# A gated recurrence and an FFT-like convolution: the small spectrum's eviction, the order of the filter's loads, and a planner's priorities

## The chip, the cores and the metric

The kernel runs on one core of one Trainium2 chip. A core has five engines with queues of their own: TensorE (PE in the profile; weight loads are PEld) multiplies matrices and writes into PSUM, VectorE (DVE) and ScalarE (ACT) work elementwise and empty PSUM, GpSimd (POOL) works elementwise on SBUF, and SyncE (SP) here only issues DMA transfers. The metric is the time of one execution on the device in microseconds (us), less being better; of several runs the median is given.

## The reference

Two layers follow each other. Inputs are `x` and `f_logit` of shape (4, 6272, 256), and all results are float32.

```python
# first layer: a gated recurrence over time, per channel
f = lower_bound + (1 - lower_bound) * sigmoid(f_logit)
h[t] = f[t] * h[t-1] + (1 - f[t]) * x[t]          # 6272 steps, 4 x 256 channels
# second layer: projections, a circular convolution along time, gating
proj = h @ w_proj                                  # 256 -> 768
x1, x2, x3 = proj[..., :256], proj[..., 256:512], proj[..., 512:]
conv = irfft(rfft(x2) * rfft(filter_fft))          # length 6272, circular
out  = (x1 * conv * x3) @ w_out                    # 256 -> 256
```

## The kernel before, in words

The transform of length 6272 = 49 x 128 is done as matmuls in two factors. The kernel has a stage that prepares constants and the filter's spectrum, and then for each of the four batches a chain of phases. All names below are the kinds by which the code calls its operations.

**Preparation (`prepare`).** The filter (6.4 MB) is loaded in 13 groups (`ff`, L612) into places that later hold other things: seven in X2, two in Hu, one in the W region of HA and two in the A region of HA, where the constants are also built. Each group is copied to a rounding type (`fr`, L333 here: ScalarE), rotated by a matmul (`rot`, L623) and evicted (`f2`, L338 here: VectorE). When all 13 are there, the first factor `FF1` (L645) runs for 16 units, its results are evicted (`afs`), the second factor `FF2` (L663) follows, is evicted (`hw`, L335) and stored as the spectrum H in DRAM (`hst`, L671). One row of each unit is treated apart: it is collected in `mX` (L654), transformed by `last` (L680) and evicted once by another `hw` (L340) into eight spare columns, 49 to 56, of each of the 128 blocks of 113 columns in X2. This is the small spectrum, Hm. W, the projection and output weights, is loaded (`wl`, L475 and L477) into parts of HA that later hold the wrapped copy of h, and is scaled and copied on ScalarE (L481, L486, L491). The arguments of all constants are computed on VectorE and go through one sine on ScalarE (L563). `warm` matmuls keep TensorE running at the start.

**The recurrence (`hgrn`),** per batch in 13 chunks of 512 steps: load f_logit and x (`load`, L361; three buffers each), sigmoid (`sig`, L364, ScalarE), product (`u`, L366, GpSimd), transposes on TensorE (`sT` and `uT`, L373), the gate `f` (L387 ScalarE, L389 VectorE) and the scan (L395, VectorE). The first 3072 steps of h are copied behind its end (`wrap`, L343).

**The convolution,** per batch: `P` (L703) projects to x2, evicted into X2 (`x2`, L338 and L333). `F1` (L716) multiplies blocks of X2 and is evicted (`A`). `F2` (L761) is multiplied with H, which is loaded anew for each of 16 units (`H`, L751, three buffers), by `prod` (L774, VectorE). `mini` (L732), `zm` (L738, reads Hm) and `slot` (L766, GpSimd) do the row treated apart. `I2` (L784) goes back and is evicted as Th. Beside this, `x13` (L422), `xs` (L434) and `z` (L438, GpSimd) make x1 times x3. Then `I1` (L817), `y` (L823), `proj` (L835), `o` (L335) and `store` (L845) finish 13 groups of the output.

**What sets the order.** The order of all instructions, their engine where two can do it, and their PSUM banks are fixed before the run by the planner (`Plan`). It goes through the operations as a simulation would, with costs written in the code, and always takes the one that can start first; among those it takes the one with the highest level, which is the longest path to the end plus a number from the table `LEAD` for its kind and batch. `SHY` adds hundredths of a microsecond to the start for one engine, and so says which of two engines is preferred. A transfer lands, for the planner, at issue plus `lag` plus `dma`. Every engine then works through its own list in that order; an instruction waits until what it needs is there.

Of the kernel before, what the change touches and what calls it, by code (L numbers as in the profile page):

```python
# [24 lines left out]
Q = 49  # L25
TB = 98
# [11 lines left out]
NU = NEP // UE  # L38
HS = 64.0 / S
# [17 lines left out]
class Plan:  # L57
# [14 lines left out]
    SHY = {("A", "ACT"): 12, ("A", "DVE"): 22, ("Th", "ACT"): -16, ("Th", "DVE"): 1259,  # L72
            ("afs", "ACT"): 15, ("afs", "DVE"): 27, ("args", "ACT"): -138, ("args", "DVE"): 197,
            ("f", "ACT"): -6, ("f", "DVE"): 55, ("f2", "ACT"): 1138, ("f2", "DVE"): -715,
            ("fr", "ACT"): -88, ("fr", "DVE"): 39, ("fr", "POOL"): 1220, ("hw", "ACT"): -64,
            ("hw", "DVE"): -15, ("o", "ACT"): -63, ("o", "DVE"): 1089, ("tabs", "DVE"): -1060,
            ("tabs", "POOL"): -660, ("wcol", "DVE"): 109, ("wcol", "SP"): -513,
            ("wrap", "ACT"): 847, ("wrap", "POOL"): 90, ("x2", "ACT"): 88, ("x2", "DVE"): 19}
# [4 lines left out]

    LEAD = {
        "A": (5, -88, -65, 49), "F1": (101, -181, 3729, -100), "F2": (143, -28, -46, -324),
        "FF1": (15, 0, 0, 0), "FF2": (-324, 0, 0, 0), "H": (-141, 0, -2, -160),
        "I1": (0, -79, -343, -1), "I2": (-27, -52, 104, -101), "P": (142, 279, -78, 130),
        "Th": (-154, 45, -110, -124), "W": (-40, 0, 0, 0), "afs": (1, 0, 0, 0),
        "args": (-199, 0, 0, 0), "f": (236, 71, 103, 350), "f2": (-8, 0, 0, 0),
        "ff": (110, 0, 0, 0), "fr": (17, 0, 0, 0), "hst": (-231, 0, 0, 0), "hw": (36, 0, 0, 0),  # L90
        "iden": (188, 0, 0, 0), "iota": (11, 0, 0, 0), "last": (-216, 0, 0, 0),
        "load": (50, 16, 0, 117), "mX": (6, 0, 0, 0), "mini": (32, -33, -31, 2),
        "o": (-13, -109, 26, 170), "pad": (-72, 0, 0, 0), "pre": (-1, 0, 0, 0),
        "prod": (22, -43, 224, -263), "proj": (-5176, -5169, -102, -470), "rest": (4, 0, 0, 0),
        "rot": (7, 0, 0, 0), "sT": (-19, -534, 184, -2177), "scan": (-8, -139, -462, -1078),
        "sig": (175, 0, -1697, 1), "slot": (180, -88, 29, 529), "store": (123, 47, -49, 43),
        "tabs": (9, 0, 0, 0), "turns": (-99, 0, 0, 0), "u": (13, 9, -123, -140),
        "uT": (-126, -29, -3660, 551), "warm": (117, 0, 0, 0), "wcol": (-49, 0, 0, 0),
        "wl": (626, 0, 0, 0), "wrap": (-165, -168, -149, -144), "x13": (-30, -3595, -282, -1865),
        "x2": (-23, 7, 7, -169), "xs": (244, -309, 414, -35), "y": (37, 82, -119, -74),  # L100
        "z": (-639, -96, -92, 0), "zm": (662, -21, 80, 112),
# [6 lines left out]
    def op(self, kind, cost, fn, r=(), w=(), dma=0.0, lag=0.0, table=None, take=0, src=None, part=None):  # L108
        preds = set()
        for t in r:  # L110
            if t in self.writer:
                preds.add(self.writer[t])
        for t in w:
            if t in self.writer:
                preds.add(self.writer[t])
            preds.update(self.readers.get(t, ()))
        me = len(self.ops)
        if src is not None:
            preds.add(src)
            self.ops[src]["users"].append(me)  # L120
        self.ops.append(dict(kind=kind, batch=self.batch, cost=cost, fn=fn, preds=preds, dma=dma, lag=lag,
                             table=table, succ=[], take=take, src=src, part=part, users=[]))
        for p in preds:
            self.ops[p]["succ"].append(me)
        for t in r:
            self.readers.setdefault(t, set()).add(me)
        for t in w:
            self.writer[t] = me
            self.readers[t] = set()
        return me  # L130
# [12 lines left out]
    def schedule(self, level):  # L143
# [3 lines left out]
        dma, table, rows, lanes = 0.0, "none", False, []  # L147
# [23 lines left out]
        uses, done, order = {}, {}, []  # L171
        while base:
# [35 lines left out]
            end[i] = t  # L208
# [20 lines left out]
        return max(end), order  # L229
# [9 lines left out]

    def emit(self):  # L240
        level = [v + self.LEAD.get(o["kind"], (0,) * 4)[o["batch"]] for v, o in zip(self.levels(), self.ops)]
        for i, e, b in self.schedule(level)[1]:
            if b is None:
                self.ops[i]["fn"](e)
            else:
                self.ops[i]["fn"](e, b)
# [3 lines left out]
def kernel(  # L250
# [101 lines left out]
    def hgrn(b):  # L352
        for c in range(NCHK):
# [6 lines left out]
            for dst, src, t in ((ft, f_logit, ("ft", k)), (xt, x, ("xt", k))):  # L360
                op("load", {"SP": 0.46}, lambda e, dst=dst, src=src, t0=t0, n=n: nc.sync.dma_start(  # L361
                    dst, src[b, t0:t0 + n, :].rearrange("(p j) d -> p j d", p=128)),
                   w=[t], dma=0.38 * nb, lag=2.4)
# [81 lines left out]
    def prepare(tmp):  # L445
# [4 lines left out]
        raws += [(HA[:, A0 + a:A0 + a + 2048], [("At", i), ("At", i + 1)]) for i, a in ((0, 0), (2, 2048))]  # L450
# [224 lines left out]
        def last(e, pb):  # L675
# [8 lines left out]
        op("hw", {"DVE": 1.5}, lambda e, pb: copy(  # L684
            e, Hm[:TB],
            PS[:TB, pb:pb + 2].rearrange("p e (a k i) -> p e a k i", a=2, k=2), HS),
# [60 lines left out]
    def unit(b, u):  # L747
# [5 lines left out]
           r=[("H", u, i) for i in range(2)], w=[("Hu", h)], dma=1.7, lag=2.0)  # L753
# [50 lines left out]
    def phase_o(b):  # L804
        for g, r0 in enumerate(range(0, Q, 4)):
# [25 lines left out]
            def proj(e, ob, yk=yk, rn=rn):  # L831
# [16 lines left out]
               r=[("osb", k)], dma=0.37 * rn, lag=1.3)  # L848
# [58 lines left out]
```

## Time and profile before

| | |
|---|---|
| median of three runs | 513.89 us (512.42 to 514.6) |
| profiled execution, its own time | 517.71 us |
| span of its profile | 515.7 us |
| busy in the span: PE, DVE, ACT, POOL | 481.4, 450.7, 411.5, 370.5 us |
| mean granted TensorE clock | 0.985 |
| DMA traffic | 116.39 MB, mean 226 GB/s |
| FF1 starts, P of batch 0, F1 of batch 0 | 30.12, 85.12, 104.94 us |
| P of batches 1, 2, 3 starts | 202.14, near 312.4, 421.61 us |

Busy shares are averages over stages with different limits; a stage is read in its own window. Matmuls are pipelined, so a busy TensorE need not be at its peak. A wait is named by the instruction that ended it.

### The profile page before, as it was taken

What the parts mean: (1) busy time and instruction counts of PE and PEld (TensorE: products, weight loads), DVE (VectorE), ACT (ScalarE), POOL (GpSimd) and SP (SyncE); (2) the same over time, 40 slices, a digit from 0 to 9 for tenths busy, and PEclk for the clock granted to TensorE, in tenths of its full rate; (3) what the DMA queues carried; (4) which work ended last, traced back from release to release, by engine and by line L of the source; (5) the groups of instructions that cost most, each with busy time, mean ns of one, the idle gap of its engine ahead of it and who ended that gap; (6) DMA issues with size and microseconds to landing.
All of it is one profiled execution on the core that took longest, in us unless ns stands there. A gap on an engine that the chain in (4) does not pass through costs nothing.

```text
span 515.7 us, 13281 instructions
## 1 busy us (share of the span) xinstructions
PE 481.4 (93%) x5257; PEld 378.8 (73%) x5257; DVE 450.7 (87%) x465; ACT 411.5 (80%) x586; POOL 370.5 (72%) x315
## 2 busy tenths in 40 slices
PE   7997998789999899999999999999999999999796
PEld 5876777666776699867667888676777987666585
DVE  7985898989999799999998997988899989989754
ACT  4995887558988987789999877999987755999554
POOL 3475875449989973599999849699996632989800
PEclk9998999989999999999999999999999999999889
DMA  8979898326667899448658996247599860344157
GB/s 305 406 240 307 275 352 292 126 67 200 205 187 242 289 316 344 172 132 274 201 173 308 332 329 265 106 156 209 173 251 292 329 245 12 107 137 136 32 215 286
DMA packets 41725, 116.39 MB, mean 226 GB/s; under 512 B 4384, under 2 KB 6304, under 8 KB 41664
## 3 DMA queue, kind: packets, MB, share of 16 engines
q1 hardware_dynamic: 41664, 115.56, 65.3%
q8 instruction: 41, 0.67, 0.5%
q14 instruction: 20, 0.16, 0.1%
HBM read 84.54 MB, written 31.00 MB: 224 GB/s over the span
## 4 chain that ended last, share of the span: by engine, by line
PE 42%; DVE 9%; DMA 9%; POOL 8%; ACT 7%; issue 4%; POOLq 0%; ACTq 0%; DVEq 0%
PE PS L422 9%; PE PS L835 7%; PE PS L373 7%; POOL zt L438 6%; PE PS L784 5%; DVE X L338 5%; PE PS L716 5%; PE PS L761 4%; DMA XT<-in_x_dram 4%; PE PS L817 3%; DMA FL<-in_f_logit_dram 2%; DMA out_dram<-osb 2%; POOL XT L366 1%; DVE PP L774 1%; DMA Hu<-H 1%
## 5 line engine op out<-in xcount | busy, mean ns | idle before, releaser
L438 POOL TENSOR_TENSOR zt<-x1s,x3s 128x490 f16<-128x490 f32 (+1 forms) x104 | 200.6, 1950 | 47.4 <-ACT x3s L434 32.9
L774 DVE TENSOR_TENSOR PP<-PS,Hu 98x1008 f16<-98x1008 f32 x128 | 146.7, 1199 | 8.3 <-PE PS L761 3.3
L366 POOL TENSOR_TENSOR XT<-XT,FL 128x1024 f32<-128x1024 f32 (+1 forms) x52 | 117.0, 2253 | 48.0 <-DMA XT<-in_x_dram 18.9
L395 DVE TENSOR_TENSOR_SCAN HA<-fTs,HA,PS 128x512 f16<-128x512 f32 (+1 forms) x96 | 114.2, 1204 | 9.8 <-ACT fTs L387 6.0
L422 PE MATMUL PS<-HA,W 128*128 128x490 f16 (+1 forms) x416 | 106.4, 369 | 2.8 <-ACT x1s L434 1.0
L387 ACT ACTIVATE fTs<-PS,nomc 128x512 f32<-128x512 f32 (+1 forms) x99 | 66.3, 675 | 11.9 <-PE PS L373 11.3
L823 DVE TENSOR_TENSOR ys<-PS,zt 128x1024 fp32r<-128x1024 f32 (+1 forms) x52 | 59.6, 1161 | 14.1 <-PE PS L817 6.5
L335 ACT ACTIVATE osb<-PS 128x1024 f32<-128x1024 f32 (+1 forms) x52 | 50.7, 976 | 26.3 <-PE PS L835 23.7
L434 ACT ACTIVATE x1s<-PS 128x490 f32<-128x490 f32 (+1 forms) x104 | 61.0, 586 | 11.7 <-POOL zt L438 8.9
L373 PE MATMUL PS<-iden,XT 128*128 128x128 f32 x392 | 62.7, 281 | 2.2 <-POOL XT L366 0.6
L835 PE MATMUL PS<-Wo,ys 128*128 128x256 f32 x392 | 61.0, 299 | 3.5 <-DVE ys L823 3.2
L364 ACT ACTIVATE FL<-FL 128x1024 f32<-128x1024 f32 (+1 forms) x52 | 52.7, 1013 | 14.1 <-DMA FL<-in_f_logit_dram 13.9
L373 PE MATMUL PS<-iden,FL 128*128 128x128 f32 x392 | 61.3, 277 | 1.6 <-ACT FL L364 1.0
L434 ACT ACTIVATE x3s<-PS 128x490 f32<-128x490 f32 (+1 forms) x104 | 61.3, 589 | 1.2 <-PE PS L422 0.8
L784 PEld LDWEIGHTS <-PP 98*128 98x128 f16 x1024 | 51.1, 98 | 11.8 <-issue 2.8
L422 PEld LDWEIGHTS <-W 128*128 128x128 f16 x416 | 35.0, 98 | 30.0 <-issue 10.7
L835 PEld LDWEIGHTS PS<-Wo,ys 128*128 128x128 f32 x392 | 51.2, 194 | 7.0 <-DVE ys L823 3.4
L338 DVE CAST X<-PS 128x1024 f16<-128x1024 f32 (+1 forms) x38 | 51.4, 1461 | 4.6 <-PE PS L703 4.4
L333 ACT CAST Th<-PS 128x784 f16<-128x784 f32 x64 | 52.5, 821 | 3.0 <-PE PS L784 2.5
L333 ACT CAST HA<-PS 128x1024 f16<-128x1024 f32 x46 | 46.6, 1026 | 9.5 <-PE PS L716 9.3
L784 PE MATMUL PS<-VA,PP 98*128 98x98 f16 x512 | 52.7, 207 | 1.2 <-DVE PP L774 1.0
L373 PEld LDWEIGHTS PS<-iden,XT 128*128 128x128 f32 x392 | 44.4, 141 | 12.3 <-issue 2.2
(99 smaller groups left out, 697.2 us busy)
## 6 DMA issues: line engine op xcount, KB each, us to landing
Hu<-H SPq DMA_DIRECT2D x64, 392.0 KB
FL<-in_f_logit_dram SPq DMA_DIRECT2D x48, 512.0 KB
XT<-in_x_dram SPq DMA_DIRECT2D x48, 512.0 KB
out_dram<-osb SPq DMA_DIRECT2D x48, 512.0 KB
X<-in_moe_filter_fft_dram SPq DMA_DIRECT2D x7, 512.0 KB
H<-Hu SPq DMA_DIRECT2D x16, 196.0 KB
H<-Hu SPq DMA_DIRECT2D x16, 128.0 KB
HA<-in_moe_filter_fft_dram SPq DMA_DIRECT2D x3, 512.0 KB
```

The costliest lines, as they stand in the source:

```text
L333: nc.scalar.copy(dst, src)
L338: nc.vector.tensor_copy(dst, src)
L366: op("u", {"POOL": 0.1 + 0.553 * nb}, lambda e, xt=xt, ft=ft: nc.gpsimd.tensor_tensor(xt, xt, ft, op=AOP.mult), r=[("ft", k)], w=[("xt", k)])
L373: nc.tensor.transpose(PS[:, p, j:128 * nb:nb], src[:, j, cols], iden[:])
L387: nc.scalar.activation(fT, PS[:, p, 0:n], AF.Identity, scale=by, bias=1.0)
L395: nc.vector.tensor_tensor_scan(h, fT, PS[:, p, 0:n], init, op0=AOP.mult, op1=AOP.add),
L422: nc.tensor.matmul(PS[:, p, 0:n], W13[:, kh, js], HA[:, HB[kh] + t0:HB[kh] + t0 + n], start=(kh == 0), stop=(kh == 1))
L434: nc.scalar.activation(xs(i), PS[:, p, 0:n], AF.Copy, scale=1.0 if i else ZS),
L438: nc.gpsimd.tensor_tensor(late["zt"][:, jb, :, m0:m0 + nm], xs(0).rearrange("p (m r) -> p r m", r=Q), xs(1).rearrange("p (m r) -> p r m", ...
L774: nc.vector.tensor_tensor(PP[:TB, k, o, :, :, 1:64], px.unsqueeze(1).broadcast_to([TB, 2, UE, 63]), hh[:, :, :, 1:64], op=AOP.mult)
L784: nc.tensor.matmul(PS[:, ib + o, pr * TB:(pr + 1) * TB], PP[:TB, k, o, n, 2 * pr:2 * pr + 2, :], v[:TB], start=(n == 0), stop=(n == 1))
L835: nc.tensor.matmul(po[:, i, :], late["ys"][:, yk, kh, i * 128:(i + 1) * 128], Wo[:, kh, :], start=(kh == 0), stop=(kh == 1))
```

## The change

The planner gets a margin and slopes. `MARGIN` is added to the landing of x, f_logit and H loads and of stores as the operations that depend on them see it. `TILT` adds to the level a number that runs from minus half to plus half over the operations of one kind and batch. The tables `SHY` and `LEAD` are replaced throughout; a higher `LEAD` means earlier. Shown are the entries that bear on the filter and the weights. The two landing places for the filter in the A region are taken away. The eviction of the small spectrum is written with eight results side by side and may go to ScalarE.

```diff
+MARGIN = 1.0
...
-    SHY = {("A", "ACT"): 12, ("A", "DVE"): 22, ("Th", "ACT"): -16, ("Th", "DVE"): 1259,
-            ("afs", "ACT"): 15, ("afs", "DVE"): 27, ("args", "ACT"): -138, ("args", "DVE"): 197,
-            ("f", "ACT"): -6, ("f", "DVE"): 55, ("f2", "ACT"): 1138, ("f2", "DVE"): -715,
-            ("fr", "ACT"): -88, ("fr", "DVE"): 39, ("fr", "POOL"): 1220, ("hw", "ACT"): -64,
...
+    SHY = {("A", "ACT"): 27, ("A", "DVE"): 27, ("Th", "ACT"): -10, ("Th", "DVE"): 779,
+            ("afs", "ACT"): 51, ("afs", "DVE"): -12, ("f", "ACT"): -4, ("f", "DVE"): 452,
+            ("f2", "ACT"): 100, ("f2", "DVE"): 126, ("fr", "ACT"): 290, ("fr", "DVE"): 2705,
+            ("fr", "POOL"): -84, ("hw", "ACT"): -32, ("hw", "DVE"): 364, ("o", "ACT"): 13,
...
     LEAD = {
...
-        "I1": (0, -79, -343, -1), "I2": (-27, -52, 104, -101), "P": (142, 279, -78, 130),
-        "Th": (-154, 45, -110, -124), "W": (-40, 0, 0, 0), "afs": (1, 0, 0, 0),
...
-        "ff": (110, 0, 0, 0), "fr": (17, 0, 0, 0), "hst": (-231, 0, 0, 0), "hw": (36, 0, 0, 0),
...
-        "load": (50, 16, 0, 117), "mX": (6, 0, 0, 0), "mini": (32, -33, -31, 2),
...
-        "wl": (626, 0, 0, 0), "wrap": (-165, -168, -149, -144), "x13": (-30, -3595, -282, -1865),
...
+        "ff": (5684, 0, 0, 0), "fr": (505, 0, 0, 0), "hst": (566, 0, 0, 0), "hw": (-475, 0, 0, 0),
...
+        "load": (1910, -587, 70, -424), "mX": (103, 0, 0, 0), "mini": (162, -443, 3560, 2034),
...
+        "turns": (-46, 0, 0, 0), "u": (801, 3, 107, 648), "uT": (10, -692, -6798, -121),
+        "warm": (-40, 0, 0, 0), "wcol": (443, 0, 0, 0), "wl": (-474, 0, 0, 0),
...
-            end[i] = t
+            end[i] = t + o["margin"]
+            last = max(last, t)
...
+    def urgency(self):
+        n, at = {}, []
+        for o in self.ops:
+            k = o["kind"], o["batch"]
+            at.append(n.get(k, 0))
+            n[k] = at[-1] + 1
+        zero = (0,) * 4
+        return [v + self.LEAD.get(o["kind"], zero)[o["batch"]]
+                + self.TILT.get(o["kind"], zero)[o["batch"]] * (j / n[o["kind"], o["batch"]] - 0.5)
+                for v, o, j in zip(self.levels(), self.ops, at)]
...
-                   w=[t], dma=0.38 * nb, lag=2.4)
+                   w=[t], dma=0.38 * nb, lag=2.4, margin=MARGIN)
...
-        raws += [(HA[:, A0 + a:A0 + a + 2048], [("At", i), ("At", i + 1)]) for i, a in ((0, 0), (2, 2048))]
...
-        op("hw", {"DVE": 1.5}, lambda e, pb: copy(
-            e, Hm[:TB],
-            PS[:TB, pb:pb + 2].rearrange("p e (a k i) -> p e a k i", a=2, k=2), HS),
+        op("hw", {"DVE": 1.15, "ACT": 0.95}, lambda e, pb: copy(
+            e, xv[:TB, :, Q:Q + 8].rearrange("p i (e c) -> p i e c", e=2),
+            PS[:TB, pb:pb + 2].rearrange("p e (c i) -> p i e c", c=4), HS),
            w=["Hm"], src=lst)
...
-           r=[("H", u, i) for i in range(2)], w=[("Hu", h)], dma=1.7, lag=2.0)
+           r=[("H", u, i) for i in range(2)], w=[("Hu", h)], dma=1.7, lag=2.0, margin=MARGIN)
...
-               r=[("osb", k)], dma=0.37 * rn, lag=1.3)
+               r=[("osb", k)], dma=0.37 * rn, lag=1.3, margin=MARGIN)
```

## The prediction

> **What bounds the kernel now.** I read the busy shares first, then the windows by stage, then the chain of waits, then the order of time where a window showed a hole.
>
> ```profile
> PE 481.4 (93%) x5257; PEld 378.8 (73%) x5257; DVE 450.7 (87%) x465; ACT 411.5 (80%) x586; POOL 370.5 (72%) x315
> ...
> PEclk9998999989999999999999999999999999999889
> ```
>
> TensorE and VectorE are both nearly full, so no single engine can be relieved alone. The TensorE clock dips in the tenths near 50, 105 and 490 us. The windows say where the loss lies (columns: length, then busy us of PE, PEld, DVE, ACT, POOL, then clock, DMA share, GB/s):
>
> ```profile
> 0.00:30.00 30.00, 25.18 (x189) 20.49 (x189) 25.11 (x66) 22.95 (x27) 14.16 (x31) 1.00 0.92 354
> 30.00:85.00 55.00, 51.11 (x375) 41.26 (x375) 44.91 (x51) 42.99 (x59) 37.13 (x42) 0.97 0.86 280
> ...
> 100.00:105.00 5.00, 0.06 (x1) 0.06 (x2) 4.88 (x2) 1.00 (x3) 1.92 (x1) 0.95 0.38 118
> 105.00:202.00 97.00, 94.11 (x1104) 72.38 (x1104) 89.47 (x85) 81.06 (x125) 81.94 (x64) 0.98 0.70 230
> ```
>
> From 105 to 421.7 us (batches 0 to 2) TensorE is idle 2.9 us up to 202, then 0.4, 1.5, 0.6 and 4.2 us: 9.6 us of 316.7. The big hole is 100 to 105. In order of time:
>
> ```profile
> 100.14 4.74 DVE L340 TENSOR_SCALAR X<-PS 98x1024 f16<-98x1024 f32 x1
> ...
> 104.94 1.89 PE L716 MATMUL PS<-D,X 128*128 128x128 f16 x16 [4.94 <-DVE X L340]
> ```
>
> The last eviction of the small spectrum takes 4.74 us where the code's cost for it is 1.5, and all of phase F1 (L716) stands behind it, because F1 reads columns of the same tile. The hole has an aftermath: the granted clock is 0.63 from 104 to 106 and 0.52 from 106 to 108.
>
> ```profile
> 5.95 1.28 ACT L486 ACT_TABLE_LOAD   x1 [5.95 <-DMA HA<-in_moe_w_proj_dram]
> ...
> 8.53 1.05 ACT L333 CAST afs<-X 128x1024 fp32r<-128x1024 f32 x1
> ...
> 27.30 0.40 ACT L333 CAST afs<-X 128x256 fp32r<-128x256 f32 x1
> ...
> 30.12 2.26 PE L645 MATMUL PS<-D1r,f 128*128 128x256 f32 x16
> ```
>
> At the start ScalarE waits for W, then makes all 13 filter copies alone, among table loads, W and the sine, until 27.7 us. Only then can the last rotation and its eviction end and FF1 (L645) start, at 30.12.
>
> **The change part by part.** All sums are against the profiled execution: span 515.7, its own time 517.71, which is 3.8 us over the median 513.89.
>
> *Eviction in runs of eight.* Before, each of 1024 two-byte results went to a place of its own, 226 bytes from the last (113 columns), with dense reads. After, eight results lie side by side and the reads hop 512 bytes in PSUM. No row has just this form; the nearest is the eviction of phase P, whose reads hop 1 KB at every element and whose writes come in runs of four:
>
> ```profile
> L338 DVE CAST X<-PS x38: 1302/1461/1683, 87.0 to 434.4; 128x1024 f16<-128x1024 f32 x34, 128x256 f16<-128x256 f32 x4
> ```
>
> Its median is 1.46 us for the same 1024 elements; dense to dense (L338 into HA) is 1.21. The Trainium skill speaks against part of the gain: "Vector Engine (DVE) Microarchitecture Reference", section 5.2, gives 1.73 ns per column for a stream whose source hops every element (1.054 dense), so by estimate 1024 x 1.73 + 75 ns = 1.85 us, and its worst row for hopping writes, 2.51 ns, would make the old form 2.6 us and the gain only 0.8. The row of 4.74 refutes the second number here. I take 1.4, between the two rows and nearer the one with hopping reads: 4.74 - 1.4 = 3.3 us (by the rule for the new form 2.9; ends 2.8 and 3.5). ScalarE may take it instead; its P eviction is 1.48, the same price. All 3.3 us lie on the path, since TensorE waited 4.94 us. With a hole of about 1.6 us the clock should stay up: from 104.94 to about 107.8 it ran at about half, which costs half of 2.9, 1.4 us. Together 4.7. If the planner puts the eviction earlier, up to 1.4 us more is hidden; If F1 is put ahead of it, the eviction waits for F1, and the first zm for the eviction.
>
> *Filter ahead of W, copies on GpSimd and ScalarE.* W (1.03 MB) no longer stands ahead of the filter (6.42 MB). From 5 us on the queues moved 400 to 430 GB/s, some 1.25 us per 0.52 MB group, and some 0.8 MB had come before. So the last full groups land near 4.5 + (6.42 - 0.8)/0.41 = 18.2 us. Two of the twelve landing places go: they lay where the constants are built and made loads wait for VectorE's arguments (until 12.8). Ten are left, and the last three loads wait for places that the first three copies free at about 6 to 9 us, before SP gets to them. What is moved back is W's two loads (issue 0.46 us each) behind the filter and perhaps the first six x and f loads. Behind W stand its seven ScalarE copies (4.3 us), then the wraps (12 of 0.62 us) and at 85 us phase P: a slack of tens of us. SP's own queue pays nothing, as the number of issues is the same. The x and f loads (first issued at 12.35) land behind the filter from about 19.5 us on; ScalarE first touched one at 24.45, so nothing is lost.
>
> The copy on GpSimd: the nearest row is L602, a dense copy of 1920 elements in 1.85 us, so 1.03 us for 1024. "GPSIMD Engine Reference", section 4.1, warns that elementwise work on GpSimd is about half as fast as on VectorE (for two inputs; nearly full rate for one); read as a warning for this copy, L538's 0.67 us for 1002 elements doubled is 1.37. By the row six copies cost 6.2 us, by the warning 8.2; GpSimd was idle 15.8 of the first 30 us, so either is covered, and I take the row. What is queued behind a copy on GpSimd is the building of the constants (1.7 us of iotas, then VectorE's arguments, the sine, D1r at 16.3): D1r is due at FF1, 6 us later, so it bears a delay. If that cover is gone, each copy waited for costs FF1 about 1.25 us. ScalarE loses about six copies, 6.3 us, of its 22.95. The 26 evictions of rotations (L338, 0.67 us, all on VectorE at 17 us) get nearly equal preference: some ten go to ScalarE, and VectorE needs about 11 us after its arguments end at 12.8. That puts the last eviction at 23 to 24 and FF1 at 23 instead of 30.1: 7 us.
>
> How much of it arrives at phase P (85.1)? Between 30 and 85 TensorE is busy 51.1 of 55, so P can come no sooner than 23 + 51 = 74. ScalarE: 22.95 + 43.0 - 6.3 + 6.7 = 66 busy by 85, with about 6 us idle at the start: 72. VectorE 70 - 6.7 = 63. DMA: 26 MB at 0.41 MB/us, 63. So TensorE sets it, with its waits on ScalarE's Hu eviction (3.2 us around 42 to 47, and the clock at 0.62 and 0.53 from 46 to 50). I keep those: P near 79, a gain of 6. What is late next is VectorE's x2 evictions after P, which only shift.
>
> *Margin and new priorities.* No instruction changes; the margin makes the planner place readers of a load 1 us later. The waits it aims at:
>
> ```profile
> POOL XT L366 <- DMA XT<-in_x_dram: 18.9, 10, 6.4
> ACT FL L364 <- DMA FL<-in_f_logit_dram: 13.9, 14, 3.2
> ```
>
> They are waits of GpSimd and ScalarE. The code plans 2.4 + 4 x 0.38 = 3.9 us from issue to landing; on the chain of waits such flights last 5.4 to 7.5. So 1 us goes in the right direction, not far enough. TensorE can win at most its 9.6 us of idleness from 105 to 421.7, and VectorE there is busy 92%. I take a fifth, 2 us; it can go from -4 to +8. The last batch, where VectorE waits 2.92 us for GpSimd's last product and the clock is 0.5 until 493, I leave as it is.
>
> Sum: 4.7 + 6 + 2 = 12.7, of which I drop 0.7 for stalls that a new order brings elsewhere: 12. Span 515.7 - 12 = 503.7; median 513.9 - 12 = 501.9.
>
> **The rivals.**
>
> *The front gain is lost:* FF1 comes earlier, but the stage to P stretches because ScalarE, with ten more evictions, becomes the bound. Then only the eviction counts: 513.9 - 4.7 = 509. For it: TensorE's longest wait in that stage, 2.6 us, is for ScalarE's Hu eviction. Against: ScalarE was busy only 34.1 of the 45 us from 40 to 85, and the sum above gives it 72.
>
> *The new order also fills the middle and the end:* half of the 9.6 us and 2 or 3 us of the last batch's hole. 501.9 + 2 (counted already) - 4.8 - 3 = 496. For it: the waits above are the planner's errors. Against: TensorE's busy share is already 97%.
>
> *Slower:* the margin becomes real delay. x and f have three buffers each, and a load is issued only when TensorE has turned the old chunk (SP waits 67.6 us for that between 105 and 421). A reader planned 1 us later frees its buffer later, once per round: 13/3 = 4.3 us per batch, 13 us in three batches; H, with three buffers and 16 loads, adds 16/3 = 5.3 in each of four, 21. If both lie on the path, 502 + 34 = 536; with about half, 520. It decides from 12 us on, that is when over a third of these delays are seen by TensorE. Against: TensorE has other work nearly everywhere.
>
> *Nothing:* F1 gets another last wait at the same time and the order is no better: 514.
>
> **How the numbers follow.** Forecast 0.55, front lost 0.15, middle and end too 0.22, nothing 0.03, slower 0.05. The likeliest gives 502. The range 494 to 510 holds the first three with their ends (eviction 2.8 to 3.5, FF1 3 to 9, order -4 to +8) and leaves out the last two and the best corner. No change is within 0.5%, 2.6 us, about what this measurement can tell: faster 0.92, same 0.03, slower 0.05.
>
> **What would show it.** The eviction near 1.4 us and F1 within 2 us of P's last eviction; the clock at 1.00 there; FF1's first matmul near 23 and P's near 79; six or seven filter copies on GpSimd at about 1.0 us; the waits for x and f under 25 us together. I am wrong if FF1 still starts after 28, if P starts after 83, or if TensorE's idleness between F1 and the last batch grows by more than 4 us.

## The result and the profile after

The changed kernel takes 507.98 us (median, 507.51 to 510.11), the one before 514.25 us on the same chip: 6.3 us less, ratio 0.9885, 95% interval 0.9836 to 0.9933. The forecast was 502.0 us. The direction held, and the time lies inside the stated range, near its upper end; the gain was half of the twelve microseconds that were worked out. The profiled execution took 508.43 us, its span is 506.6 us. A few single executions lay in a slower state, over 1.5% above the fastest of the same kernel, and the medians given here leave them out.

The busy shares and the granted clock on the page of the kernel after:

```profile
PE 481.4 (95%) x5257; PEld 375.4 (74%) x5257; DVE 443.9 (88%) x451; ACT 411.1 (81%) x587; POOL 386.5 (76%) x328
...
PEclk9999999899999999999999999999999999999889
```

TensorE's busy time in these two profiles is the same 481.4 us; only its idle time has shrunk. ScalarE's share hardly moves and GpSimd has 16 us more. The clock's dip near 105 us is gone, and a shallower one stands near 90.

The windows by stage of the kernel after (length, busy us of PE, PEld, DVE, ACT, POOL, then clock, DMA share, GB/s). FF1 starts at 26.43 and P of batch 0 at 91.06, so the second row is now the stretch up to P:

```profile
0.00:30.00 30.00, 26.15 (x199) 21.67 (x201) 23.87 (x54) 15.61 (x22) 26.31 (x43) 1.00 0.92 355
30.00:91.00 61.00, 54.50 (x384) 40.71 (x383) 51.05 (x55) 45.86 (x63) 39.99 (x43) 0.98 0.90 289
102.00:106.00 4.00, 3.75 (x27) 2.13 (x26) 3.57 (x3) 2.79 (x6) 2.72 (x2) 1.00 0.00 0
106.00:197.00 91.00, 89.93 (x1091) 69.09 (x1089) 85.89 (x82) 81.44 (x123) 78.21 (x63) 1.00 0.74 247
```

The hole ahead of F1 is closed at full clock. ScalarE's load in the first 30 us fell from 22.95 to 15.61 us and GpSimd's rose from 14.16 to 26.31. And yet the stretch to P is longer than before.

The order of time in the kernel after (start, duration, engine, line): an eviction of the filter's spectrum into Hu and, behind it, the small spectrum's; a matmul that waits for the first of them; eight matmuls of x13 (L450); P's first matmul and F1's.

```profile
85.71 1.02 ACT L363 ACTIVATE Hu<-PS 98x1024 f16<-98x1024 f32 x1 [1.73 <-DMA H<-Hu]
86.63 1.20 ACT L363 ACTIVATE X<-PS 98x1024 f16<-98x1024 f32 x1
...
86.78 0.70 PE L690 MATMUL PS<-afs,FTr 64*98 64x512 f32 x4 [1.83 <-ACT Hu L363]
...
87.88 3.18 PE L450 MATMUL PS<-HA,W 128*128 128x490 f16 x8
...
91.06 0.42 PE L730 MATMUL PS<-W,HA 128*128 128x256 f16 x1
...
105.63 1.51 PE L743 MATMUL PS<-D,X 128*128 128x128 f16 x24 [0.23 <-DVE X L366]
```

The eviction takes 1.20 us instead of 4.74. It moved to ScalarE and ahead of P, and F1 now waits 0.23 us for its last input instead of 4.94. The block also shows a wait just ahead of P: ScalarE waits 1.73 us until a store of H has freed Hu, TensorE waits 1.83 us behind it, and the granted clock is 0.54 from 88 to 90 and 0.60 from 90 to 92 us. That is the dip near 90.

The filter copies, GpSimd's constants and products, and then VectorE's instructions up to the first scan, each in order of time:

```profile
11.44 4.93 POOL L371 CAST afs<-X 128x1024 fp32r<-128x1024 f32 x3 [1.29 <-PE PS L650]
...
16.32 1.04 POOL L371 CAST afs<-Hu 128x1024 fp32r<-128x1024 f32 x1
...
29.04 0.43 POOL L599 TENSOR_SCALAR FTr<-PP,cols 128x49 fp32r<-128x49 f32 x1
29.43 4.68 POOL L394 TENSOR_TENSOR XT<-XT,FL 128x1024 f32<-128x1024 f32 x2
...
5.90 3.35 DVE L573 SCALAR_TENSOR_TENSOR HA<-HA,cols 128x98 f32<-128x98 f32 x4
...
13.53 1.95 DVE L588 TENSOR_TENSOR PP<-HA,PP 128x1032 f32<-128x1032 f32 x1
...
29.67 4.46 DVE L494 TENSOR_SCALAR omc<-wcol 128x2 f32<-128x2 f32 x1
34.04 0.15 DVE L496 TENSOR_SCALAR nomc<-wcol 128x2 f32<-128x2 f32 x1
35.01 1.22 DVE L423 TENSOR_TENSOR_SCAN HA<-fTs,PS 128x512 f16<-128x512 f32 x1 [0.81 <-ACT fTs L415]
```

All thirteen copies went to GpSimd, not half of them. Most of the full ones take 1.04 to 1.13 us; three that ran beside VectorE's long instructions took 4.93 us together, and VectorE's last one for the arguments took 1.95 us where before it was 1.23. Behind the copies come the constants until 29.4 us, and only then the first product x times sigmoid (26.52 before). VectorE's instruction on two columns took 4.46 us and ended when the two GpSimd products that ran beside it, one right behind the other, had ended (29.43 + 4.68 = 34.11); the first scan began at 35.01, where before it was 30.15.

The waits of the kernel after (us in all, times, longest):

```profile
POOL XT L394 <- DMA XT<-in_x_dram: 13.6, 7, 7.0
...
ACT Hu L363 <- DMA H<-Hu: 6.6, 7, 1.7
...
ACT FL L392 <- DMA FL<-in_f_logit_dram: 5.4, 7, 1.5
```

The two that the margin aims at fell from 32.8 to 19.0 us together (38.5 and 45.3 in the two runs of the old order with the new eviction, 21.7 and 23.4 in the other two runs of the new one). A third one, for the stores of the filter's spectrum H, rose from 2.6 us.

### The profile page after: what moved, and what is told of

Same layout as the page of the kernel before. It is cut to its first block, busy times and chain, and to the rows that moved or that the text cites. A ratio compares the mean times of both kernels' runs of the same rounds, so it can differ in the third digit from the quotient of the medians.

```text
span 506.6 us, 13245 instructions
## 1 busy us (share of the span) xinstructions
PE 481.4 (95%) x5257; PEld 375.4 (74%) x5257; DVE 443.9 (88%) x451; ACT 411.1 (81%) x587; POOL 386.5 (76%) x328
## 4 chain that ended last, share of the span: by engine, by line
PE 63%; DVE 10%; DMA 8%; issue 6%; ACT 6%; POOL 5%; SPq 0%; POOLq 0%; ACTq 0%; DVEq 0%
PE PS L450 11%; PE PS L401 10%; PE PS L862 9%; PE PS L730 8%; PE PS L811 5%; DMA H<-Hu 5%; PE PS L743 5%; PE PS L788 4%; PE PS L844 4%; POOL zt L466 4%; PE PS L621 3%; DVE PP L801 3%; DVE HA L423 2%; DMA FL<-in_f_logit_dram 2%; DVE X L366 2%
## 5 line engine op out<-in xcount | busy, mean ns | idle before, releaser
L450 PE MATMUL PS<-HA,W 128*128 128x490 f16 (+1 forms) x416 | 107.7, 371 | 1.5 <-DVE PP L801 1.0
L415 ACT ACTIVATE fTs<-PS,nomc 128x512 f32<-128x512 f32 (+1 forms) x104 | 69.4, 669 | 18.8 <-PE PS L401 13.2
L450 PEld LDWEIGHTS <-W 128*128 128x128 f16 x416 | 35.0, 98 | 27.5 <-issue 9.7
L811 PE MATMUL PS<-VB,PP 98*128 98x98 f16 x512 | 52.1, 207 | 0.0
L366 DVE CAST X<-PS 128x1024 f16<-128x1024 f32 (+1 forms) x34 | 47.0, 1487 | 5.2 <-PE PS L730 3.9
```

Source lines behind the costliest of these rows:

```text
L366: nc.vector.tensor_copy(dst, src)
L415: nc.scalar.activation(fT, PS[:, p, 0:n], AF.Identity, scale=by, bias=1.0)
L450: nc.tensor.matmul(PS[:, p, 0:n], W13[:, kh, js], HA[:, HB[kh] + t0:HB[kh] + t0 + n], start=(kh == 0), stop=(kh == 1))
L811: nc.tensor.matmul(PS[:, ib + o, pr * TB:(pr + 1) * TB], PP[:TB, k, o, n, 2 * pr:2 * pr + 2, :], v[:TB], start=(n == 0), stop=(n == 1))
```

## The experiments

Positions in time are starts of the first matmul in the profiled execution of each kernel (the 85.12 given for P of batch 0 ahead of the prediction is its first weight load). P of batch 1 is the yardstick for the front with batch 0, because all orders have done the same matmuls by then; at P of batch 0 they have not (after's order has more of the gates' `x13` done). Likewise the distance from P of batch 1 to P of batch 3.

| kernel | median us | ratio to before [95%] | FF1 | P, batch 0 | P, batch 1 | P1 to P3 |
|---|---|---|---|---|---|---|
| before | 514.25 | | 30.12 | 85.23 | 202.14 | 219.5 |
| evict_only | 508.86 | 0.9849 [0.978, 0.992] | 29.79 | 81.84 | 194.40 | 222.7 |
| evict_only_more | 509.87 | 0.9899 [0.986, 0.994] | 29.65 | 80.40 | 192.79 | 220.1 |
| after | 507.98 | 0.9885 [0.984, 0.993] | 26.43 | 91.06 | 196.57 | 216.6 |
| after_again | 506.92 | 0.9813 [0.975, 0.988] | 26.42 | 90.38 | 196.40 | 218.0 |
| after_third | 507.46 | 0.9845 [0.981, 0.989] | 26.36 | 88.63 | 195.19 | 217.9 |
| old_evict | 512.31 | 0.9965 [0.993, 1.000] | 26.07 | 92.05 | 198.09 | 217.6 |
| old_evict_more | 511.78 | 0.9939 [0.991, 0.997] | 26.37 | 95.43 | 202.06 | 216.4 |
| fr_act | 512.46 | 0.9926 [0.990, 0.995] | 34.87 | 96.09 | 201.40 | 216.8 |
| w_first | 507.94 | 0.9845 [0.980, 0.989] | 27.42 | 90.54 | 196.13 | 215.9 |
| wcol_first | 504.25 | 0.9762 [0.969, 0.983] | 29.11 | 89.47 | 194.28 | 216.2 |
| wcol_first_more | 507.57 | 0.9844 [0.981, 0.988] | 27.46 | 89.10 | 195.31 | 217.9 |
| both_first | 507.44 | 0.9845 [0.979, 0.990] | 28.11 | 91.52 | 198.76 | 216.1 |
| early | 505.86 | 0.9834 [0.977, 0.990] | 28.39 | 90.37 | 195.83 | 216.5 |
| splice | 505.66 | 0.9807 [0.977, 0.985] | 29.94 | 81.03 | 194.62 | 216.2 |
| light | 503.75 | 0.9785 [0.973, 0.984] | 26.43 | 86.88 | 191.69 | 216.6 |

The rows of one and the same kernel show how far such numbers carry: medians differ by 1 to 3.3 us from one session to the next, P of batch 1 by 1 to 4 us.

### The eviction by itself

evict_only is the kernel before with the new addresses of the eviction and nothing else, so the same order, on VectorE. after_again is the changed kernel on the same chip.

```diff
-            e, Hm[:TB],
-            PS[:TB, pb:pb + 2].rearrange("p e (a k i) -> p e a k i", a=2, k=2), HS),
+            e, xv[:TB, :, Q:Q + 8].rearrange("p i (e c) -> p i e c", e=2),
+            PS[:TB, pb:pb + 2].rearrange("p e (c i) -> p i e c", c=4), HS),
```

> The kernel before with only the eviction of the small spectrum written in runs of eight; planned cost, order and engine (VectorE) as before. My sum: it takes 1.4 us instead of 4.74, F1 of batch 0 starts near 101.5 instead of 104.9, the clock stays up, and the time falls by 4.7 us (0.9%). Then most of what the whole change brought is this eviction. Rival: ScalarE or the next H loads fill the hole, so that F1 comes earlier but P of batch 1 does not: less than 1.5 us.

> The changed kernel itself, on the same chip as the three runs beside it, for comparison. Both theories: 1.0 to 1.4% under the kernel before, F1 of batch 0 near 105.6 us, P of batch 0 near 91.1.

The order of time in evict_only:

```profile
96.79 1.19 DVE L340 TENSOR_SCALAR X<-PS 98x1024 f16<-98x1024 f32 x1
...
98.03 1.07 PE L716 MATMUL PS<-D,X 128*128 128x128 f16 x16 [1.37 <-DVE X L340]
```

4.74 us became 1.19, TensorE's wait 4.94 became 1.37, and P to F1 16.2 us instead of 19.7. This edit of two lines brings most of what the whole change brings. F1 came at 98.03 and not at the 101.5 forecast, because P of batch 0 came 3.4 us earlier as well, and that the edit can't have done: the eviction lies behind P. The waits from 25 to 105 us say where it comes from, first in before, then in evict_only:

```profile
ACT FL L364 <- DMA FL<-in_f_logit_dram: 4.2, 3, 3.2
PE PS L645 <- ACT Hu L335: 3.2, 2, 2.6
```

```profile
ACT FL L364 <- DMA FL<-in_f_logit_dram: 2.8, 2, 1.7
PE PS L645 <- ACT Hu L335: 0.6, 1, 0.6
```

In the profiled execution of before one load of f_logit landed late. ScalarE stood idle 3.17 us for it until 43.24, TensorE then 2.59 us until 45.26 for the Hu eviction behind it, and the clock was 0.62 and 0.53 from 46 to 50. The three other profiles of this order (evict_only, evict_only_more and splice, below) have no such stall; their clock is 1.00 there, and P of batch 0 starts at 80.4 to 81.8 instead of 85.23. So of the 8.2 us between P of batch 1 in before (202.14) and their mean (193.94) about half is that one late load. From P of batch 0 to P of batch 1 before takes 116.9 us and these three 112.9 on the mean: 4.1 us is what the eviction is worth by stages. Once more, beside a variant of the changed kernel (wcol_first_more, below):

> Before with the new eviction alone, once more. If the new order brings 2 us of its own, as the medians so far say: 508 to 510, 0.985 to 0.989 of before. If the eviction alone brings all: 506.5 to 508.

It took 509.87 us, against 507.57 us for wcol_first_more on the same chip; evict_only took 508.86, against 506.92 for after_again. So the order seems to have a small worth of its own, some 2 us, though the intervals of each pair overlap.

The reverse is old_evict: the changed kernel with the two lines put back, on ScalarE and ahead of P, and once more beside after_third on one chip.

> After with the eviction of the small spectrum in its old form (128 elements apart, runs of one), everything else as in after, so on ScalarE and ahead of P. Theory A (in after's order the eviction lies beside P's matmuls and its duration is nearly free): the eviction takes 4.5 to 5 us, P to F1 stays within 1.5 us of after's 14.6, time 506.5 to 508.5, at most 1.5 us over after_again's 506.92. Rival E (the eviction is on the path in this order too): 510 to 512.

> After with the old form of the eviction once more. Theory A (in the new order its duration lies beside matmuls of P): at most 2 us over after_third of the same call. Rival E (it costs what it cost in the old order): 4 to 6 us over it.

> The changed kernel itself, for comparison on the same chip: 506 to 508.5.

Theory A, that the eviction is nearly free in the new order, fell. It costs 511.78 - 507.46 = 4.3 us, and P of batch 1 comes 4.0 us later on the mean of the profiles (200.1 against 196.05). The order of time, first old_evict_more, then after_third:

```profile
87.18 4.77 ACT L363 ACTIVATE X<-PS 98x1024 f16<-98x1024 f32 x1
...
92.00 3.42 PE L450 MATMUL PS<-HA,W 128*128 128x490 f16 x8 [3.59 <-ACT X L363]
```

```profile
85.63 1.19 ACT L363 ACTIVATE X<-PS 98x1024 f16<-98x1024 f32 x1
...
86.87 1.81 PE L450 MATMUL PS<-HA,W 128*128 128x490 f16 x8
```

With the old form TensorE waits 3.59 us for it in this order too. The eight matmuls behind it take 3.42 us instead of 1.81, but this part is not the old form's alone: in after itself, with the new form, the same eight took 3.18 us (above). The theory looked only at what reads the small spectrum (F1, far off), not at what is queued behind the instruction on ScalarE and behind that on TensorE.

### Tables, margin and slopes one at a time: four plans that told nothing of them

Four kernels let the planner plan anew with one input changed. front_before uses the old tables, preferences, landing places and no margin up to the first P, and the new ones behind; front_after is the reverse.

```diff
-                    c += self.SHY.get((o["kind"], e), 0) / 100
+                    old = front
+                    c += (self.SHY_B if old else self.SHY).get((o["kind"], e), 0) / 100
...
-            end[i] = t + o["margin"]
+            end[i] = t + (0.0 if front else o["margin"])
```

> A hybrid: up to the first P the planner uses the tables of the kernel before (no slopes, no margin, twelve landing places for the filter), from there on those of the changed kernel with slopes and margin; the new eviction is in it, on VectorE. Theory A: the change is a sum of an eviction (about 5 us gained), a front that became 5 to 6 us longer, and a middle that became about 7 us shorter; then this kernel has P of batch 0 near 82 to 85 and batches 1 and 2 (P of batch 1 to P of batch 3) in about 217 us, and its time is 500 to 503 us, below the changed kernel. Theory B: the middle is short only because the new front had already done 18 groups of x13 before F1 of batch 0; then the time is 505 to 508.

> The opposite hybrid: front as in the changed kernel, from the first P on the tables of the kernel before without slopes and margin. Theory A: P of batch 0 near 91, batches 1 and 2 in 219 to 223 us, and 512 to 516 us, no better than the kernel before. Theory B: 506 to 509, since what the front did ahead is what counts.

margin0 sets the margin to nothing, tilt0 the slopes, with all tables as in the changed kernel:

```diff
-MARGIN = 1.0
+MARGIN = 0.0
```

```diff
-                + self.TILT.get(o["kind"], zero)[o["batch"]] * (j / n[o["kind"], o["batch"]] - 0.5)
+                + self.TILT.get(o["kind"], zero)[o["batch"]] * (j / n[o["kind"], o["batch"]] - 0.5) * 0.0
```

> The changed kernel planned with a margin of 0 instead of 1 us, all tables kept. If the margin is what shortens the middle: GpSimd's and ScalarE's waits for x and f grow from 19 us to over 30, batches 1 and 2 take 2 to 5 us longer. If it is idle: within 1.5 us of the changed kernel either way. If it is real delay (the rival): 2 us or more shorter.

> The changed kernel with all slopes at zero, tables and margin kept. If the slopes are what shortens the middle: 3 to 8 us above the changed kernel. If the other tables do it: within 1.5 us.

They took 556.03, 535.18, 550.57 and 528.34 us, far from every theory. The longest waits of margin0 and then of tilt0:

```profile
POOL PP L793 <- DVE zp L765: 61.3, 5, 20.7
```

```profile
POOL PP L793 <- DVE zp L765: 34.5, 5, 23.6
```

GpSimd stands up to 23.6 us at a time for VectorE, because one of its instructions was put into its list too early. With each of these four other inputs the same tables give a poor order. So these runs say nothing of what the margin or the slopes are worth, and the runs that follow keep a finished order and move single instructions in it.

### Where the front goes: copies, lower_bound, W

fr_act keeps after's order and makes the thirteen copies on ScalarE:

```diff
         for i, e, b in self.schedule(level)[1]:
+            if self.ops[i]["kind"] == "fr":
+                e = "ACT"
```

> The changed kernel with its order kept, but the 13 filter copies on ScalarE as in the kernel before. Theory A: GpSimd's copies slowed VectorE's arguments (the groups from the first scaled table to the last subtraction took about twice as long as before) and pushed the constants and the first product back; without them the arguments end near 12.8 instead of 15.5 and the first product starts 3 to 6 us earlier, but ScalarE, which also has ten evictions of rotations, brings FF1 to 29 or later; P of batch 0 within 2 us of 91.1. Theory B (only FF1's start counts for P): P later by as much as FF1, 2.5 to 4 us, and the time 2.5 to 4 us above the changed kernel.

FF1 comes 8.4 us later (34.87), P of batch 1 5.4 us and the end 5.5 us. So in this order GpSimd is the right place for the copies, which neither theory had in that size (and the first product did not start earlier, as theory A had it: 30.67 against 29.43). The order of time on VectorE in fr_act shows the price that GpSimd's copies have on the other side:

```profile
5.90 1.00 DVE L575 SCALAR_TENSOR_TENSOR HA<-HA,cols 128x98 f32<-128x98 f32 x4
```

These four instructions for the arguments take 1.00 us; beside GpSimd's copies in after they took 3.35 (above).

wcol_first loads lower_bound first on SP and makes omc and nomc directly behind the arguments, so that VectorE need not stop for them when the recurrence starts:

```diff
-        for i, e, b in self.schedule(level)[1]:
+        first, scale = [o for o, k in zip(order, kind) if k == "wcol"]
+        rest = [o for o, k in zip(order, kind) if k != "wcol"]
+        at = 1 + max(n for n, o in enumerate(rest) if self.ops[o[0]]["kind"] == "args" and o[1] == "DVE")
+        for i, e, b in [first] + rest[:at] + [scale] + rest[at:]:
```

> The changed kernel with its order kept, except that the load of lower_bound is SP's first instruction and the two scalings that use it (omc, nomc) follow VectorE's arguments instead of coming at 29.7 us. Theory A: the front lost its gain because these two came late and VectorE then stood 4.46 us behind GpSimd's product, so that the first gate and scan came at 35.0 instead of about 32.5, and the evictions of FF1 stood behind them: P of batch 0 moves from 91.1 to 87 to 89 and the time falls by 2 to 4 us against the changed kernel. Theory B: the stage up to P is bound by what TensorE, ScalarE and the H stores can do, and the late start is made up for: P within 0.7 us of 91.1, the time the same.

The first time it took 504.25 us and the theory seemed shown. The second time it took 507.57 us:

> After's order with lower_bound's load first and omc and nomc behind the arguments, once more. Theory A (VectorE's wait for omc was on the path of the first gates, worth 2 to 3 us): 503.5 to 505.5, 0.975 to 0.981 of before. Rival (the earlier 504.25 was scatter of four runs): 506.5 to 508, as after.

The 504.25 was scatter, or most of it. The wait of 4.46 us is real, and in the repeat it is gone as well, but taking it away gives at most some 1 us at P of batch 1 (195.31 against 195.2 to 196.6).

early also moves GpSimd's constants behind the first two products:

```diff
+        move("wcol", 0, "ff", -1)
+        move("wcol", 1, "tabs", 2)
+        move("rest", 0, "u", 1)
```

> After's order of work with three moves: the load of lower_bound goes behind the thirteen filter loads on SP's queue (in wcol_first it was the very first), omc and nomc come on VectorE behind the three tables, and GpSimd's block of constants (5.5 us) goes behind the first two products x*sigmoid instead of ahead of them. Theory A (the front's length is set by when the recurrence gets going): first matmul of FF1 at 26 to 27, first scan at 32.5 to 34 (after: 35.0), first matmul of P at 86 to 88, time 501 to 503, 1 to 3 us under wcol_first's 504.25. Rival T (the front is bound by throughput between 45 and 85 us, TensorE 95% busy there, and an earlier start is only waited away): P at 89 to 90 as in wcol_first and a time of 504 to 505. The prediction's own step (FF1 plus 51 us is P): P at 77 to 78.

The first product started at 26.27 instead of 29.43 and the first scan at 34.15 instead of 35.01; P of batch 0 was at 90.37. Theory A's 86 to 88 fell, and the rival's 89 to 90 is the nearer. The test is not a clean one: of the 3.2 us at the first product only 0.9 reached the first scan, and FF1 came 2 us later in this run (28.39).

w_first issues W's loads ahead of the filter again; both_first does that and has lower_bound first:

```diff
+        loads = [o for o in order if self.ops[o[0]]["kind"] == "wl"]
+        for i, e, b in loads + [o for o in order if o not in loads]:
```

> After's order with one move: the loads of W and of the output weights are issued ahead of the filter's again. Prediction's step (the filter ahead of W brings 6 us to the first matmul of P): FF1 at 29 to 30, P at 96 to 97, time 512 to 513. Theory A (FF1's start isn't what P waits for; the recurrence and the copies are): FF1 2 to 4 us later than after's 26.43, P at 91 to 93, time 507 to 509.

> After's order with lower_bound's load first and W's and the output weights' behind it, all three ahead of the filter as in before; omc and nomc behind the arguments. Theory (the place of W's loads is worth nothing, that of lower_bound 2 to 3 us): P of batch 1 at 193.5 to 195, time 503.5 to 505.5. The prediction's step (the filter has to be ahead of W): P of batch 1 at 198 or later, time 508 or more.

w_first took 507.94 us, the same as the changed kernel, with FF1 only 1 us later and P of batch 1 at 196.13. The place of W's loads shows no worth in it. both_first missed its theory: P of batch 1 came at 198.76, where the rival had it, and the time was 507.44, the same as after and just under the rival's 508. One profile with P so late, beside w_first's 196.13, is within the 4 us by which such positions scatter.

### The old front with the new middle

splice plays a written-out list: before's order with the new eviction up to P of batch 1, after's order from there on.

```diff
-        for i, e, b in self.schedule(level)[1]:
+        order = [(int(i), names[int(w[0])], int(w[1]) if w[1:] else None)
+                 for i, w in (o.split(".") for o in ORDER.split())]
+        for i, e, b in order:
...
+        raws += [(HA[:, A0 + a:A0 + a + 2048], [("At", i), ("At", i + 1)]) for i, a in ((0, 0), (2, 2048))]
```

> Before's order of work, with the new eviction, up to the first matmul of P of batch 1; from there on after's order. Theory A (the new order costs some 2 us in the front and brings some 6 us in batches 1 and 2): first matmul of P of batch 1 at 194 to 195 as in evict_only (after: 196.6), from there to P of batch 3 216 to 217.5 us as in after (evict_only: 222.7), time 502.5 to 504.5. Rival W (the gain of the order belongs to the order as one whole and doesn't come with a part of it): P1 to P3 220 to 223 us and a time of 507 to 509.

Both stages came out as theory A had them: P of batch 1 at 194.62 as in the old order, then 216.2 us to P of batch 3 as in the new one. The time, 505.66 us, is 1.2 over the forecast's upper end. So the new order's gain sits behind batch 0, and the front before was no worse than the front after. The windows of batch 2 show the gain, first before, then after:

```profile
312.40:421.60 109.20, 104.03 (x1211) 83.00 (x1209) 97.60 (x91) 92.34 (x135) 86.12 (x67) 1.00 0.67 219
```

```profile
307.20:413.20 106.00, 105.32 (x1227) 83.84 (x1226) 99.27 (x93) 93.32 (x136) 87.34 (x67) 1.00 0.69 238
```

TensorE was idle 5.2 us there and is idle 0.7 us now. In batch 1 it went from 1.5 to 3.9 us the other way.

### What holds the front

light keeps every instruction of the changed kernel, but loads only the first half of batch 0's x and f_logit tiles from the fourth on, so that batch 0's values are not those of the reference:

```diff
-                    dst, src[b, t0:t0 + n, :].rearrange("(p j) d -> p j d", p=128)),
+                m = nb // 2 if b == 0 and c >= NX and nb > 1 else nb
+                    dst[:, 0:m], src[b, t0:t0 + n, :].rearrange("(p j) d -> p j d", p=128)[:, 0:m]),
```

> After, but of batch 0's tiles of x and f_logit from the fourth on only the first half is loaded (the other half keeps what the tile held, so batch 0's values are not the reference's); every instruction stays, 18 transfers of 512 KB become 256 KB, 4.6 MB less, some 13 us of all 16 engines at the 340 to 370 GB/s that the front shows. Theory D (the DMA engines hold the front): the waits of ScalarE for the stores of H (6.6 us in after) fall under 3 us, first matmul of P of batch 1 at 188 to 193 instead of 196.6, time 500 to 504. Rival T (TensorE's work and the recurrence hold it, the transfers only fill): P of batch 1 within 1 us of 196.6, time 506 to 508.5.

Theory D held in all three numbers. The windows up to P, first of after, then of light:

```profile
0.00:26.00 26.00, 22.66 (x173) 18.88 (x174) 20.87 (x49) 14.14 (x21) 22.40 (x36) 1.00 0.95 370
26.00:87.00 61.00, 54.02 (x398) 41.87 (x397) 53.57 (x59) 43.94 (x60) 43.77 (x50) 1.00 0.88 279
```

```profile
26.00:87.00 61.00, 55.96 (x413) 43.09 (x411) 54.47 (x61) 46.30 (x64) 43.76 (x50) 1.00 0.70 216
```

And the wait for the stores of H in light, 6.6 us in after:

```profile
ACT Hu L363 <- DMA H<-Hu: 1.3, 2, 1.0
```

With the DMA engines' share at 0.70 instead of 0.88, P of batch 1 comes 4.4 us earlier (191.69 against 196.05 on the mean of three) and the kernel takes 503.75 us, against 507.46 for after_third on the same chip. 4.6 MB less are 0.18 x 61 = 11 us of all 16 engines, so less than half of that reaches the end: TensorE, busy 76.7 of the first 87 us, is close behind. The wait just ahead of P shows the way that it takes: TensorE's 1.83 us for the Hu eviction are 0.41 here, the clock stays up, and the eight matmuls of x13 take 1.81 us instead of 3.18. Half a load also lands sooner than a whole one; whether the bytes in all or the landing of each is what counts, light does not part.

## Why the prediction was half right

**The eviction: right.** Forecast 1.4 us and 4.7 in all; it takes 1.19 on VectorE and 1.20 on ScalarE. Its worth was 4.3 us in the new order on one chip, 4.7 and 7.0 in the old, and 4.1 by stages. The 1.85 us estimated from the Trainium skill ("Vector Engine (DVE) Microarchitecture Reference", section 5.2) was too high: its rows are of four-byte streams in SBUF, and here reads that hop 512 bytes in PSUM cost nothing beside the 1.21 us of a dense eviction of 1024 elements. The clock at F1 stayed at 1.00, as forecast.

**The front: this step failed.** "So TensorE sets it ... P near 79, a gain of 6." P of batch 0 came at 91.06, past the 83 that the prediction itself had named as a sign of being wrong. FF1 did start earlier, by 3.7 us rather than 7, and nothing of it arrived: with the new eviction in both, the old front reaches P of batch 1 at 193.9 (mean of evict_only, evict_only_more and splice, 192.8 to 194.6) and the new one at 196.05 (three runs of after, 195.2 to 196.6), 2.1 us later. Four terms of that sum were wrong.

The first is FF1 "at 23". All thirteen copies on one engine end at 23.5 us, the rotation and the evictions behind the last one at 26.3; the copies and VectorE's arguments held each other up, so that the arguments ended at 15.5 instead of the 12.8 that the sum took over from before.

The second is the stage's length. "I keep those" kept a wait of 3.2 us and the half clock from 46 to 50 that came of one late load in the profiled execution (above). Without it this order has P at 80.4 to 81.8, so that "near 79" would have been a gain of some 2 us and not of 6.

The third is "DMA: 26 MB at 0.41 MB/us, 63". The 0.41 was the best rate of the first stretch. Up to 87 us the engines moved 26 x 370 + 61 x 279 = 26.6 MB, and were full for 0.95 x 26 + 0.88 x 61 = 78.4 us. A stage's DMA time is its share times its length, not its bytes by the best rate: before's own rows, shown in the prediction, have 0.92 x 30 + 0.86 x 55 = 75 us of 85. Those rows stood there, and they say that the transfers were as near to being the bound as TensorE (busy 76 us of the 85). In evict_only they were full for 0.94 x 26 + 0.89 x 56 = 74 of the 82 us up to P. 75 us would by themselves still have allowed P at 79; but they leave 4 us of slack, not 16, and then a late transfer is felt. light shows that it is: fewer bytes, the same instructions, 4.4 us earlier.

The fourth is that FF1's start was carried on to P as if nothing else began the stage. In the eight profiles of after's order in which FF1 starts between 26.4 and 29.1, with the new eviction and all bytes, P of batch 1 starts between 194.3 and 198.8, and the earlier FF1 does not go with the earlier P: the latest FF1 (29.11) has the earliest P of batch 1. Only a start 8 us later (fr_act, which also loads ScalarE with the copies) is felt. "SP's own queue pays nothing" and "it bears a delay" were too light as well: lower_bound's load slid from 0.74 to 18.62 us with W's, and the first product waited behind GpSimd's copies and constants until 29.43. wcol_first_more undoes the one and early a part of the other, and neither brings more than the scatter, so nothing shows that they are the cause.

The traces show one difference of the size of the 2.1 us. Up to 92 us TensorE waits 2.9, 3.2 and 2.0 us for Hu evictions of ScalarE in the three runs of after, and 0.6, 0.4 and 0.5 us in evict_only, evict_only_more and splice: 2.2 us more on the mean. ScalarE in turn waits for H's stores, 6.6, 5.4 and 5.8 us against 3.1, 2.6 and 3.1. That is an account and not a test: no run moved these stores alone, and why they hold ScalarE longer in the new order stays open.

**GpSimd's copy: right in price, wrong in number.** 1.04 us for one alone, as the row of before said, and not the 1.37 that came of doubling VectorE's time. "GPSIMD Engine Reference", section 4.1, of the Trainium skill gives the factor of two for two inputs and roughly the line rate for one; a copy has one, so the page and the row agree. The forecast had six or seven of them, the planner gave all thirteen. What was not weighed is what they and VectorE's instructions do to each other.

**Margin and priorities: right in direction, a little small.** Forecast 2 us. From P of batch 1 to P of batch 3 the old order takes 220.8 us (219.5, 222.7, 220.1) and the new 217.5 (216.6, 218.0, 217.9): 3.3. In the profiles of before and after TensorE's idle time in that stretch fell by 2.1 us. The waits for x and f fell to 19.0 us, under the 25 named. How much of it is the margin's and how much the slopes' stays open, since no run could part them. Behind P of batch 3 nothing changed (to the end of the span 92.7 us as the mean of before and the two of evict_only, 92.5 as that of the three of after).

**The sum.** Eviction -4.3, front +2.1, batches 1 and 2 -3.3: -5.5 from the stages, where 6.3 was measured. The forecast said -4.7, -6 and -2. That the total still lay in the range is in part luck: the order behind the front brought 1.3 us more than forecast. Of the rivals, "the front gain is lost", at 509 us with a chance of 0.15, was the case, but not for its reason: ScalarE, busy 58 of the first 87 us, did not become the bound by its work. TensorE's longest wait was for its Hu eviction, as that rival had noted, and this one waited for the stores of H. "Slower" by real delay of the margin didn't happen.

No version here was shown to beat the changed kernel. splice and early lie 2 us below it, within the scatter of the runs.

## What to carry to other kernels

Before a start is pulled forward, add up each resource's full time over the whole stage that follows, for the DMA queues as share times length; if one of them is near the stage's length, the earlier start is likely to be waited away. Look at the stage in a second execution before its length goes into a sum: a single late load had lengthened this one by some 4 us. The smallest part of a large change can be the one that pays: one instruction with a scattered destination, seen as a hole in the order of time, was worth more than all the new tables together. When a planner's tables are tuned, test its parts by moving instructions in the finished order and not by planning anew, and repeat a gain of 3 us before believing it.

## What was not expected of the hardware

A VectorE instruction on SBUF operands did not end before GpSimd's work beside it: 4.46 us for 128 x 2 elements beside two GpSimd products in after, the second right behind the first, and 0.17 us in early, where GpSimd was between two copies. Beside GpSimd's copies four 128 x 98 operations took 3.35 us instead of 1.00. It goes the other way too: three copies that take 1.04 us each alone took 4.93 us together beside VectorE's long instructions.

The destination's stride set the price of the eviction on both engines: 4.74 us on VectorE and 4.77 on ScalarE for 1024 two-byte results 226 bytes apart, 1.19 and 1.20 us with eight side by side, though the reads then hop.
